# Opening order of an attention and two-MLP kernel: Q in one transfer, eight biased exponentials on ScalarE, halves of the last turned results

## The chip, the cores and the metric

The kernel runs on one core of a Trainium2 chip. The metric is the device time of one execution in microseconds, the lower the better; of several runs the median is given.

## The reference

Three layers follow one another. `q`, `k` and `v` have shape 4×8×768×64 (4 sequences, 8 heads), `mem_k` and `mem_v` 4×8×8×64; the first MLP has weights 512×2048 and 2048×512, the second the same sizes and one `alpha` for each hidden unit.

```python
for c in range(nc):                       # chunks of 32 queries
    c_start = c * chunk
    c_end = c_start + chunk
    l_start = max(0, c_start - left_ctx)  # 16 keys to the left
    r_end = min(S, c_end + right_ctx)     # 8 to the right
    k_full = np.concatenate([mem_k, k_ctx], axis=2)
    v_full = np.concatenate([mem_v, v_ctx], axis=2)
    scores = scale * np.matmul(q_c, k_full.transpose(0, 1, 3, 2))
    scores = scores - np.max(scores, axis=-1, keepdims=True)
    a = np.exp(scores)
    a = a / (np.sum(a, axis=-1, keepdims=True) + 1e-09)
    out[:, :, c_start:c_end] = np.matmul(a, v_full)
...
h = x @ w_in                              # 3072 x 512 by 512 x 2048
g = np.maximum(h, 0.0) + np.log1p(np.exp(-np.abs(h)))
x = (g @ w_out)
...
g = np.maximum(h, 0.0) + alpha * np.minimum(h, 0.0)
return (g @ w_out)
```

## The kernel before

**Attention.** The 3072 rows (sequence by position) are cut into 24 tiles of 128 rows; a tile is four chunks of 32 queries, for all 8 heads. Tiles 0 to 3 make the first block of 512 rows, tiles 4 to 7 the second; these eight are the *early* tiles, and tiles 8 to 23 (`few` in the code) are loaded in another way. One tile t goes through these steps, whose numbers stand behind the letters in what follows (s3 is the scores of tile 3):

- load of Q and K (`load_q`, `load_k`, into a room `qk`) and of V (`load_v`, six transfers: two halves of the columns, each from three ranges of rows, the memory's among them); all of them from the queue of SyncE (SP);
- q: for early tiles the heads of Q are put in the order that the scores want (`a_order`, two copies on ScalarE, here qa and qb). Half of each operand has to be zero, since two heads share a multiplication (the host lays Q out with these zeros); before the change `others` fills that half with `memset` (on VectorE for tile 0, on GpSimd for the other early tiles);
- s: 32 small matrix products on TensorE into the PSUM bank `ps_s`;
- m: the row maximum on VectorE (`a_max`, `nm`); then either the shift by it on VectorE (`a_shift`) and e, the exponential of 128×512 on ScalarE (`a_exp`), or, where a switch asks for it, `a_bias` on VectorE (the negative maximum, 128×8) and `a_shifted_exp`, eight exponentials of 128×64 on ScalarE, each with its own bias;
- the sum, the reciprocal and w, the share of each key (`a_share`, on VectorE or GpSimd);
- t: four transposes on TensorE into `ps_t`, and pt, their copies to SBUF on ScalarE;
- x: 32 products with V into `ps_x`, and from there xh on ScalarE and xl on VectorE: the two parts, high and low, into which each fp32 operand of the MLPs is split so that three fast products make one exact one.

**First MLP.** It goes by groups of one block and 128 hidden units: H (`pe_h`) is 12 matrix products of 128×512 into `ps_hh`; ScalarE computes ta and the high part of g (`act_first`, `high`), VectorE its low part (`low`); O (`pe_out`) is 12 products into `ps_o`. For the exponentials of the attention and for ta ScalarE loads different tables (ACT_TABLE_LOAD). The weights come in 512 KB rooms `raw`, and each is split into high and low parts: wh on ScalarE, wl on VectorE or GpSimd.

**Second MLP.** It is done by seven products in place of eight of quartered matrices (`quad`, `second`, bank `ps_q`); at the end VectorE turns results (`flip`: a transpose of each half and four stores).

**What sets the order.** For the first part `schedule` describes each step as a task of a `Plan` (engine, estimated microseconds, a due time, what it needs, what rooms it takes); `Plan.run` lists the tasks by due time as engines come free. The due times come from a table of numbers `O`, which also holds switches (`by0`, `by1`: GpSimd computes shares; `ca0`, `ca1`: the biased exponentials for tiles 0 to 3 and 4 to 7; `wld`: how many early wl go to VectorE). Each engine then runs its instructions strictly in that order (`InOrder`), and the same holds for loads: a load is an instruction in the queue of the engine that issues it. In the built program each load carries one of eight semaphores (DMAHW0 to DMAHW7), and a load waits on its issuing engine until an earlier load on that semaphore has landed.

Of the kernel before, what the change touches and what calls it, by code (L numbers as in the profile page):

```python
# [31 lines left out]
QN = 2 * NPAIR * P  # L32
# [48 lines left out]

PLAN = []
RUNS = 8
O = {'qo': 19.43, 'km': 103.61, 's': 132.4, 'm': 86.98, 'c': -51.87, 'e': 175.6, 'n': -19.49, 'r': -46.35, 'w': -19.52, 't': 95.77, 'pt': 85.42, 'v': 4.11, 'xh': -85.13, 'xl': -37.52, 'first': 4.43, 'gap': 13.49, 'second': 13.8, 'gap2': 10.89, 'raw': 76.14, 'ab': -97.97, 'cl': -24.77, 'ca': -41.63, 'cb': -28.14, 'cc': -52.39, 'wh': 1.69, 'wl': -37.29, 'odd': 61.8, 'sp': 29.0, 'hi': -84.66, 'lo': 120.66, 'out': 14.22, 'wait': 0.06, 'sloads': 10.35, 'qo0': 31.77, 'qo1': 59.63, 'km0': 45.44, 'km1': -1.09, 's0': 33.53, 's1': 68.06, 'm0': 99.26, 'm1': -29.86, 'c0': 87.42, 'c1': 86.99, 'e0': -47.46, 'e1': 46.23, 'n0': 20.17, 'n1': -4.91, 'r0': 23.19, 'r1': -6.49, 'w0': -81.15, 'w1': -23.28, 't0': 107.79, 't1': -40.96, 'pt0': 0.74, 'pt1': -5.53, 'v0': -87.68, 'v1': 71.52, 'xh0': -18.53, 'xh1': -22.32, 'xl0': 2.53, 'xl1': 34.49, 'by0': 3.34, 'by1': 1.01, 'va': -80.0, 'vb': -248.8, 'vc': -188.24, 'vd': -121.62, 'ra': -92.44, 'rb': -99.39, 'rc': -59.46, 'wld': -3.93, 'dra': -16.84, 'qpd': -4.87, 'ca0': 0.43, 'ca1': -2.85}


class Plan:
# [16 lines left out]
    def run(self):  # L104
# [10 lines left out]
        while left:  # L115
            able, first = [], 1e9
            for name, since in ready.items():
                engine, us, due, _, _, take, _, _ = left[name]
                t = max(since, free.get(engine, 0.0) if engine else 0.0, now)
                if engine == "SP":  # L120
                    t = max(t, free.get("DMA", 0.0) - 4.0)
                for r in set(take):
                    short = take.count(r) - rooms[r]
                    if short > 0:
                        later = sorted(u for u, g in back if g == r)
                        t = max(t, later[short - 1] + self.LAG if len(later) >= short else 1e9)
                able.append((t, due, name, engine))
            t, _, chosen, engine = min(able, key=lambda x: x[:2])
            if engine == "DMA":
                chosen = min((x for x in able if x[3] == "DMA"), key=lambda x: ready[x[2]])[2]  # L130
            if t >= 1e9:
                PLAN[:] = [x[:4] for x in order]
                raise ValueError([x[2] for x in able])
            now = t
            if engine and engine != "DMA":
                near = [x for x in able if x[3] == engine and x[0] < t + O["wait"]]
                if engine == "PE" and self.beside(last_pe):
                    near = [x for x in near if self.beside(x[2])] or near
# [12 lines left out]
            for u, g in [x for x in back if x[0] <= t]:
                rooms[g] += 1
                back.remove((u, g))
            if tab and tab != table:
                us, table = us + 1.3, tab
            if engine == "PE":
                if self.beside(name) and self.beside(last_pe):
                    us -= 0.24
                last_pe = name
                if t < 90.0 and t - free.get("PE", 0.0) > 0.5:  # L160
                    self.idle[name] = (max(free.get("PE", 0.0), came), t)
            if engine == "DVE" and free.get("POOL", 0.0) > t:
                us += 0.25 * min(us, free["POOL"] - t)
            done[name] = t + us
            if engine:
                free[engine] = t + us
            back += [(t + us, g) for g in give]
            order.append((t, us, engine, name, work))
            for a in then.get(name, ()):
                wants[a] -= 1  # L170
                if not wants[a]:
                    ready[a] = max(done[b] for b in left[a][4]) + self.LAG
# [4 lines left out]
def attention_mlp_mlp_kernel(ctx: ExitStack, tc, qk, v, w1, w2, consts, out):  # L177
# [159 lines left out]
    def load_q(t, e, c=None):  # L337
        part = slice(e * D, (e + 1) * D)
        rows = qk[t][part, :QN].rearrange("p (n e k) -> p n e k", e=2, k=D)[:, :, e]
        if c is None:  # L340
            sp.dma_start(out=raw_q[t][part].rearrange("p (n k) -> p n k", k=D), in_=rows)
        else:
            sp.dma_start(out=own(q_t[t], e)[:, c], in_=rows[:, :, c * CHUNK:(c + 1) * CHUNK])

# [9 lines left out]
        else:  # L354
            v_t[t] = apool.tile([P, 2 * DM], F32, tag="v", name="v", bufs=1)

    def load_v(t):
        for u, to, at, n in (
            (0, 0, MEM0, NMEM), (0, NMEM, 0, KW - NMEM), (0, KW, CHUNK, KW),
            (1, 0, 0, KW), (1, KW, SW - KW + NMEM, KW - NMEM), (1, 2 * KW - NMEM, MEM0 - D, NMEM),  # L360
        ):
            part = slice(u * DM, (u + 1) * DM)
            sp.dma_start(out=v_t[t][to:to + n, part], in_=v[t][at:at + n, part])

    def a_order(t, e, other=False):

        (dve.tensor_copy if other else act.copy)(out=own(q_t[t], e), in_=raw_q[t][e * D:(e + 1) * D].rearrange("p (n c k) -> p c n k", c=2, k=CHUNK))

    score_ps, turned, x_ps, part_of = {}, {}, {}, {}

# [395 lines left out]
            result(1, part)  # L766
            turn(c[:, 1, part], 1, 2 * h, 2, (lambda o, i: act.copy(out=o, in_=i), dve.tensor_copy)[h], (act, sp)[h])

    def flip(c, b, d):

        rows = out[b * N2:(b + 1) * N2, d * HK:(d + 1) * HK].rearrange("(c i) (m a j) -> m a i c j", i=32, m=2, j=32)
        for m in range(2):
            o = c[:, m, :].rearrange("p (c i) -> p c i", i=32)
            dve.transpose(out=o, in_=o)
            for a in range(4):
# [7 lines left out]
    def second(p, todo):  # L783
# [34 lines left out]
        for n in range(7 * NQ):  # L818
# [42 lines left out]
                    later.pop(0)()  # L861
            elif later:
                later.pop(0)()
            if (i, q) in ((4, 7), (5, 6), (6, 5)):
                d, b = ((0, 1), (1, 1), (0, 0))[i - 4]
                flip(c.pop((d, b)), 2 * p + b, d)
            for piece in todo.get(n, ()):
                piece()
            if 7 * NQ - n in (12, 8, 4, 1):
# [37 lines left out]
    def schedule(when):  # L907
# [5 lines left out]
        def nothing():  # L913
            pass

        def dma(name, issue, move, due, work, after=(), take=(), give=(), eng="SP"):
            add(("i",) + name, eng, issue, due, work, after, take)
            add(("x",) + name, "DMA", move, due, nothing, [("i",) + name])
            add(name, "", 2.0, due, nothing, [("x",) + name], [], give)

        for n, k in enumerate(order):
            f = k // 2
# [12 lines left out]
        for i, (b, f, first, final) in enumerate(steps):  # L935
# [10 lines left out]
            if final:  # L946
# [5 lines left out]
                for m in range(4):  # L952
                    by_act = m % 2 == 0 or f < HALF and O["dra"] > 0.5
                    add(("dr", i, m), "ACT" if by_act else "DVE", 0.65, t + 12.6, lambda i=i, m=m, b=b, by_act=by_act: drain_one(0 if by_act else 1, acc[b][m], staged[i][:, m, :]), [("db", i)], [], ["acc"])
                    dma(("dd", i, m), 1.1 if adds else 0.4, 1.0 if adds else 0.8, t + 16, lambda i=i, m=m, b=b, adds=adds: drain_to(m, staged[i][:, m, :], b, adds),
                        [("dr", i, m)], eng="POOL" if adds else "SP")
# [9 lines left out]
        def tile(t, prev, due, step=None):  # L966
# [12 lines left out]
            soon = -100 + 2 * t if start else due - O["sloads"]  # L979
            add(("qr", t), "", 0.0, soon, room, free_qk, qrooms)  # L980
            def load(c=None):
                for e in range(2):
                    load_q(t, e, c)
            if few:
                for c in range(2):
                    dma(("q", t, c), 1.5, 0.9, soon, lambda c=c: load(c), [("qr", t)] + ([("i", "q", t, c - 1)] if c else []))
            else:
                dma(("qk", t, 2), 1.45, 2.7, soon, lambda: (load(), load_k(t)), [("qr", t)])
            kafter = [("i", "q", t, 1)]
            if few:  # L990
# [190 lines left out]
```

## Time and profile before

| | |
|---|---|
| device time, 3 runs | 1090.9 us median (1090.0 to 1092.84) |
| the profiled execution | 1089.11 us, of which the span is 1087.1 us |
| mean granted clock of TensorE | 0.994 |
| TensorE busy | 1066.3 us, 98% of the span |
| VectorE / ScalarE / GpSimd busy | 717.6 / 559.7 / 232.9 us |

The span goes from the first to the last instruction that the profiler recorded; what lies around it (2.0 us here) is start and end. The profile has no program lines that help (each operation passes through line 71), so its rows are told apart by the names of the tiles. In the rows v is the room of a tile's shares and operands (it holds ordered Q, then the shifted scores and V), `word` the weight on its way to its parts, `SPq` the queue of SyncE.

### The profile page before, as it was taken

Reading aid. Unit: us, or ns where it says so; the run is one execution under the profiler, and the core shown is the slowest. Engines: PE = TensorE matmul, PEld = TensorE weight load, DVE = VectorE, ACT = ScalarE, POOL = GpSimd, SP = SyncE. Lnnn points to the kernel's source line nnn. Section 1 sums busy time; section 2 is a strip of 40 time slices with the busy share of each in tenths; the row PEclk is TensorE's granted clock in tenths of the full one; section 3 lists DMA queues with packets and bytes.
Section 4 is the critical chain, followed back from the end, with each engine's and each line's share of the span. In section 5 each row is a group of like instructions: output and inputs, shape, how many; then the busy total and the mean of one; then the engine's idle time right before and its main releaser. Section 6 shows DMA issues by size and latency. Waiting matters only on the chain.

```text
span 1087.1 us, 16452 instructions
## 1 busy us (share of the span) xinstructions
PE 1066.3 (98%) x6003; PEld 874.6 (80%) x6003; DVE 717.6 (66%) x1150; ACT 559.7 (51%) x974; POOL 232.9 (21%) x281
## 2 busy tenths in 40 slices
PE   7799999999999999999999999999999999999998
PEld 4578878888888888888888888888888888888886
DVE  6799989566644544444358166778666779666976
ACT  5654335465563554353244355765455665456543
POOL 4444444424123332223233400000000000000000
PEclk9899999999999999999999999999999999999999
DMA  9955674768644465444356373799874999856904
GB/s 225 234 152 185 167 187 121 187 164 215 186 127 151 153 197 137 167 118 151 111 194 225 134 304 113 293 276 318 201 275 174 335 300 255 239 223 252 370 1 78
DMA packets 173839, 214.53 MB, mean 197 GB/s; under 512 B 96064, under 2 KB 125888, under 8 KB 166848
## 3 DMA queue, kind: packets, MB, share of 16 engines
q1 hardware_dynamic: 169456, 196.59, 56.6%
q0 software_dynamic: 4032, 16.78, 7.9%
q8 instruction: 47, 0.77, 0.3%
q14 instruction: 32, 0.26, 0.1%
q10 hardware_dynamic: 272, 0.13, 0.0%
HBM read 154.74 MB, written 46.14 MB: 185 GB/s over the span
## 4 chain that ended last, share of the span: by engine, by line
PE 94%; DVE 3%; DMA 2%; SPq 1%; ACT 0%; issue 0%; DVEq 0%; ACTq 0%
PE ps_q L71 41%; PE ps_o L71 24%; PE ps_hh L71 24%; PE ps_x L71 2%; PE ps_s L71 2%; DVE word L71 1%; DMA raw<-in_w_dram 1%; PE ps_t L71 1%; SPq L71 1%; DMA wout<-out_ops 1%; DMA qk<-in_qk_dram 0%; DVE sm L71 0%; DVE x L71 0%; DVE nm L71 0%; DVE v L71 0%
## 5 line engine op out<-in xcount | busy, mean ns | idle before, releaser
L71 PE MATMUL ps_hh<-x,wsplit 128*128 128x512 f32 x1152 | 280.2, 392 | 0.6 <-DVE x L71 0.5
L71 PE MATMUL ps_o<-g,wsplit 128*128 128x512 f32 x1152 | 279.4, 391 | 0.8 <-ACT ta L71 0.7
L71 PEld LDWEIGHTS ps_o<-g,wsplit 128*128 128x128 f32 x1152 | 215.0, 188 | 46.5 <-ACT ta L71 1.1
L71 PEld LDWEIGHTS ps_hh<-x,wsplit 128*128 128x128 f32 x1152 | 214.5, 188 | 45.7 <-DVE x L71 0.8
L71 PE MATMUL ps_q<-g,wout 128*128 128x512 f32 x1008 | 229.3, 389 | 0.1
L71 PE MATMUL ps_q<-xop,win 128*128 128x512 f32 x1008 | 229.2, 389 | 0.0
L71 PEld LDWEIGHTS ps_q<-g,wout 128*128 128x128 f32 x1008 | 189.1, 188 | 39.8 <-ACT gb L71 0.5
L71 PEld LDWEIGHTS ps_q<-xop,win 128*128 128x128 f32 x1008 | 189.2, 188 | 39.4
L71 DVE TENSOR_TENSOR g<-ta,g 128x512 fp32r<-128x512 f32 x96 | 71.8, 748 | 132.3 <-ACT g L71 132.1
L71 ACT CAST g<-gb 128x512 fp32r<-128x512 f32 x168 | 100.8, 622 | 88.5 <-PE ps_q L71 64.6
L71 DVE TENSOR_TENSOR g<-gb,g 128x512 fp32r<-128x512 f32 x168 | 114.3, 687 | 37.9 <-ACT g L71 36.2
L71 ACT CAST g<-ta 128x512 fp32r<-128x512 f32 x96 | 59.6, 621 | 147.8 <-PE ps_o L71 147.6
L71 ACT ACTIVATE ta<-ps_hh 128x512 f32<-128x512 f32 x96 | 57.4, 598 | 106.3 <-PE ps_hh L71 101.9
L71 DVE SCALAR_TENSOR_TENSOR word<-raw,word 128x512 int32<-128x512 int32 x128 | 106.3, 831 | 2.5
L71 ACT ACTIVATE tp<-gb 128x512 f32<-128x512 f32 x48 | 30.4, 633 | 91.8 <-DVE gb L71 91.8
L71 POOL TENSOR_TENSOR wst<-wsum,wst 128x512 fp32r<-128x512 f32 x32 | 42.3, 1321 | 124.6 <-ACT wst L71 124.6
L71 POOL DMA_DIRECT2D gb<-gb x12 | 10.5, 874 | 263.6 <-DVE g L71 176.1
L71 DVE TENSOR_SCALAR word<-word 128x512 f32<-128x512 f32 (+1 forms) x128 | 65.0, 512 | 1.8
L71 POOL TENSOR_TENSOR wsplit<-word,wsplit 128x512 fp32r<-128x512 f32 x32 | 48.9, 1531 | 64.7 <-ACT wsplit L71 58.1
L71 DVE SCALAR_TENSOR_TENSOR gb<-gb,tp 128x512 f32<-128x512 f32 x48 | 33.2, 692 | 44.0 <-ACT tp L71 44.0
L71 POOL TENSOR_TENSOR wst<-word,wst 128x512 fp32r<-128x512 f32 (+1 forms) x32 | 37.6, 1176 | 110.7 <-ACT wst L71 110.7
L71 DVE TENSOR_SCALAR word<-raw 128x512 int32<-128x512 int32 x64 | 39.0, 610 | 32.0 <-POOL wst L71 13.6
(81 smaller groups left out, 930.9 us busy)
## 6 DMA issues: line engine op xcount, KB each, us to landing
wout<-out_ops SPq DMA_DIRECT2D x42, 1024.0 KB
raw<-in_w_dram SPq DMA_DIRECT2D x64, 512.0 KB
win<-in_ops SPq DMA_DIRECT2D x24, 1024.0 KB
win<-in_ops SPq DMA_DIRECT2D x24, 768.0 KB
out_ops<-wst SPq DMA_DIRECT2D x56, 256.0 KB
in_ops<-wst SPq DMA_DIRECT2D x24, 512.0 KB
gb<-gb POOLq DMA_DIRECT2D x12, 1024.0 KB, 13.5
v<-in_v_dram SPq DMA_DIRECT2D x48, 128.0 KB
```

Of the source, the lines that this page charges most:

```text
L71: i = getattr(self.engine, name)(*args, **kw)
```

## The change

The table `O` is replaced, and with it the order of the first part; of its switches four change their effect: tiles 4 to 7 take the eight biased exponentials on ScalarE in place of shift and one exponential; the shares of tiles 4 to 7 go to VectorE, not GpSimd; the first four wl go to VectorE, not GpSimd; and the six V loads of tiles 2 and 7 are issued from ScalarE's queue. For early tiles Q is loaded with one transfer of 128×1024 numbers (512 KB, the zeros that the host laid out included) where two transfers of 64×8×64 (128 KB each) brought the numbers alone; `others` is no longer called, and `a_order` copies 128×512 in place of 64×512. Some of the planner's costs differ. At the end the last turned result of each pair of blocks is stored in halves, two steps earlier.

```diff
-O = {'qo': 19.43, ..., 'by0': 3.34, 'by1': 1.01, ..., 'wld': -3.93, ..., 'ca0': 0.43, 'ca1': -2.85}
+O = {'qo': 1.94, ..., 'by0': 1, 'by1': 0, ..., 'wld': 4, ..., 'ca0': 0, 'ca1': 1, ..., 'vq2': 1, ..., 'vq7': 1, 've': 19.65}
...
-            if engine == "DVE" and free.get("POOL", 0.0) > t:
-                us += 0.25 * min(us, free["POOL"] - t)
+            if engine == "DVE":
+                us *= 0.88
+                if free.get("POOL", 0.0) > t:
+                    us += 0.3 * min(us, free["POOL"] - t)
...
-            raw_q[t] = room[:, :QN // 2]
+            raw_q[t] = room[:, :QN]
...
-            sp.dma_start(out=raw_q[t][part].rearrange("p (n k) -> p n k", k=D), in_=rows)
+            sp.dma_start(out=raw_q[t], in_=qk[t][:, :QN])
...
-    def load_v(t):
+    def load_v(t, queue):
...
-            sp.dma_start(out=v_t[t][to:to + n, part], in_=v[t][at:at + n, part])
+            queue.dma_start(out=v_t[t][to:to + n, part], in_=v[t][at:at + n, part])
...
-        (dve.tensor_copy if other else act.copy)(out=own(q_t[t], e), in_=raw_q[t][e * D:(e + 1) * D].rearrange("p (n c k) -> p c n k", c=2, k=CHUNK))
+        (dve.tensor_copy if other else act.copy)(out=q_t[t][:, e], in_=raw_q[t].rearrange("p (n c k) -> p c n k", c=2, k=CHUNK)[:, e])
...
-            if (i, q) in ((4, 7), (5, 6), (6, 5)):
-                d, b = ((0, 1), (1, 1), (0, 0))[i - 4]
-                flip(c.pop((d, b)), 2 * p + b, d)
+            for at, half, d, b in ((39, 0, 0, 1), (39, 1, 0, 1), (46, 0, 1, 1), (46, 1, 1, 1), (50, 0, 0, 0), (51, 1, 0, 0)):
+                if n == at:
+                    flip(c[d, b], 2 * p + b, d, [half])
...
-            dma(("v", t), 2.9, 2.0, (O["va"], O["vb"], O["vc"], O["vd"])[t] if start else due - 24, lambda: load_v(t), [("vr", t)])
+            by_act = not few and O["vq%d" % t] > 0.5
+            dma(("v", t), 3.0, 2.0, (O["va"], O["vb"], O["vc"], O["vd"])[t] if start else due - (24 if few else O["ve"]), lambda: load_v(t, act if by_act else sp), [("vr", t)], eng="ACT" if by_act else "SP")
...
-                add(("qz", t), "POOL" if t else "DVE", 1.5 if t else 1.1, (-50, 0)[t > 0] + t, lambda: others(q_t[t], pool if t else dve), [("vr", t)])
```

SyncE, from the program's start, before. The rooms qk_97 to qk_100 are those of tiles 0 to 3, v_119 that of tile 0:

```order
L71 DMA qk_97<-in_qk_dram 64x8x64 x2
L71 DMA qk_97<-in_qk_dram 128x4x160
L71 DMA qk_98<-in_qk_dram 64x8x64 x2
L71 DMA qk_98<-in_qk_dram 128x4x160
L71 DMA cst<-in_consts_dram 128x144
L71 DMA qk_99<-in_qk_dram 64x8x64
L71 DMA qk_99<-in_qk_dram 64x8x64 [waits DMAHW0_49]
L71 DMA qk_99<-in_qk_dram 128x4x160 [waits DMAHW1_49]
```

The same place of the changed kernel, as far as the first weights (`raw`); v_117 is the room of tile 0:

```order
L71 DMA qk_97<-in_qk_dram 128x1024
L71 DMA qk_97<-in_qk_dram 128x4x160
L71 DMA qk_98<-in_qk_dram 128x1024
L71 DMA qk_98<-in_qk_dram 128x4x160
L71 DMA cst<-in_consts_dram 128x144
L71 DMA qk_99<-in_qk_dram 128x1024
L71 DMA qk_99<-in_qk_dram 128x4x160
L71 DMA qk_100<-in_qk_dram 128x1024
L71 DMA qk_100<-in_qk_dram 128x4x160 [waits DMAHW0_49]
...
L71 DMA v_117<-in_v_dram 8x512 [waits DMAHW6_49]
L71 DMA raw<-in_w_dram 128x512 [waits DMAHW7_49]
```

A tile's Q and K are two instructions now, not three, and the first `raw` waits for the load on DMAHW7, which is Q of tile 3 (the eighth load).

ScalarE, from the exponential of tile 0 on, before:

```order
L71 ACTIVATE v_119<-v_119 128x512 [waits DVE_49,PE_49]
L71 COPY v_171<-qk_98 64x16x32 [waits DMAHW4_49]
L71 COPY v_196<-qk_99 64x16x32 [waits DMAHW7_49]
L71 COPY v_196<-qk_99 64x16x32 [waits DMAHW0_49]
L71 COPY pt<-ps_t 64x8x32 [waits PE_49]
L71 COPY pt<-ps_t 64x8x32 x3
L71 COPY v_255<-qk_100 64x16x32 [waits DMAHW2_49]
L71 ACTIVATE v_171<-v_171 128x512 [waits DVE_49]
```

And in the changed kernel (v_203 is tile 2, v_163 tile 1, v_223 tile 3):

```order
L71 ACTIVATE v_117<-v_117 128x512 [waits DVE_49,PE_49]
L71 DMA v_203<-in_v_dram 8x512 [waits DMAHW1_49]
L71 DMA v_203<-in_v_dram 56x512 [waits DMAHW3_49]
L71 DMA v_203<-in_v_dram 64x512 [waits DMAHW5_49]
L71 DMA v_203<-in_v_dram 64x512 [waits DMAHW7_49]
L71 DMA v_203<-in_v_dram 56x512 [waits DMAHW1_49]
L71 DMA v_203<-in_v_dram 8x512 [waits DMAHW3_49]
L71 COPY v_203<-qk_99 128x512
L71 ACTIVATE v_163<-v_163 128x512 [waits DVE_49,PE_49,Activation_49]
L71 COPY v_203<-qk_99 128x512
L71 COPY v_223<-qk_100 128x512
L71 COPY pt<-ps_t 64x8x32 [waits PE_49]
```

Six loads of V now stand ahead of the exponential of tile 1. The fourth of them waits on DMAHW7 for the first `raw`; the fifth and the sixth wait on DMAHW1 and DMAHW3 for the first and the second of the six themselves.

ScalarE, ahead of the second block's tiles, before: the exponential of tile 4 (v_357) is one instruction.

```order
L71 ACTIVATE v_357<-v_357 128x512 [waits DVE_49,PE_49,Activation_49]
L71 ACT_TABLE_LOAD
L71 ACTIVATE ta<-ps_hh 128x512 [waits PE_49]
L71 CAST g<-ta 128x512 [waits Activation_49]
L71 COPY v_483<-qk_419 64x16x32 [waits DMAHW3_49]
L71 COPY v_483<-qk_419 64x16x32 [waits DMAHW4_49]
```

The same place of the changed kernel (v_339 is tile 4, v_399 tile 5, v_483 tile 6, v_544 tile 7):

```order
L71 ACTIVATE v_339<-ps_s,nm 128x64 [waits DVE_49,PE_49,Activation_49]
L71 ACTIVATE v_339<-ps_s,nm 128x64 x7
L71 DMA v_544<-in_v_dram 8x512 [waits DMAHW0_49,Pool_49]
L71 DMA v_544<-in_v_dram 56x512 [waits DMAHW2_49]
L71 DMA v_544<-in_v_dram 64x512 [waits DMAHW4_49]
L71 DMA v_544<-in_v_dram 64x512 [waits DMAHW6_49]
L71 DMA v_544<-in_v_dram 56x512 [waits DMAHW0_49]
L71 DMA v_544<-in_v_dram 8x512 [waits DMAHW2_49]
L71 COPY v_483<-qk_376 128x512
L71 ACTIVATE v_399<-ps_s,nm 128x64 [waits DVE_49,PE_49,Activation_49]
L71 ACTIVATE v_399<-ps_s,nm 128x64 x7
```

Eight exponentials stand for one, and behind them the six loads of V of tile 7, the fifth and sixth again behind the first and second of their own. TensorE's order hardly differs: in both kernels all eight early tiles, four H and one O come ahead of the second O, and from there on the order is the same kind of alternation.

## Rows read from the trace of the kernel before

**Rows 1.** Windows: stretch, us, then busy time of PE, PEld, DVE, ACT, POOL, PEclk, DMA share, GB/s.

```profile
10.00:20.00 10.00, 6.68 (x134) 5.76 (x134) 5.62 (x13) 6.45 (x13) 4.23 (x15) 0.83 1.06 246
40.00:50.00 10.00, 6.34 (x74) 5.30 (x73) 7.15 (x17) 6.08 (x11) 1.98 (x4) 0.66 0.97 243
70.00:80.00 10.00, 10.00 (x46) 8.27 (x45) 9.54 (x15) 3.23 (x6) 4.18 (x3) 1.00 0.48 156
1000.00:1060.00 60.00, 60.00 (x267) 49.64 (x266) 50.25 (x82) 30.93 (x54) 0.00 (x0) 1.00 0.50 203
```

**Rows 2.** Timeline of TensorE: start, us, work, count, idle time before and its releaser.

```profile
34.20 2.83 PE L71 MATMUL ps_hh<-x,wsplit 128*128 128x512 f32 x11 [0.54 <-DVE x L71]
44.47 1.11 PE L71 MATMUL ps_t<-cst,v 128*128 128x128 f32 x4 [3.39 <-POOL v L71]
59.71 0.66 PE L71 MATMUL ps_t<-cst,v 128*128 128x128 f32 x4
65.11 3.00 PE L71 MATMUL ps_hh<-x,wsplit 128*128 128x512 f32 x12
68.04 1.15 PE L71 MATMUL ps_x<-pt,v 128*64 128x64 f32 x32
69.12 1.19 PE L71 MATMUL ps_o<-g,wsplit 128*128 128x512 f32 x4
```

**Rows 3.** Timeline of ScalarE.

```profile
3.82 0.62 ACT L71 COPY v<-qk 64x512 f32<-64x512 f32 x1 [1.79 <-DMA qk<-in_qk_dram]
9.52 0.63 ACT L71 ACTIVATE v<-v 128x512 f32<-128x512 f32 x1 [2.13 <-DVE v L71]
15.19 1.51 ACT L71 COPY pt<-ps_t 64x256 f32<-64x256 f32 x4 [3.12 <-PE ps_t L71]
17.26 0.62 ACT L71 ACTIVATE v<-v 128x512 f32<-128x512 f32 x1
37.40 1.28 ACT L71 ACT_TABLE_LOAD   x1
38.70 0.60 ACT L71 ACTIVATE ta<-ps_hh 128x512 f32<-128x512 f32 x1
```

**Rows 4.** Timeline of SyncE's queue: when its loads are issued, and for how long.

```profile
0.75 4.06 SPq L71 DMA_DIRECT2D qk<-in_qk_dram  x6
9.66 3.04 SPq L71 DMA_DIRECT2D v<-in_v_dram  x6
```

**Rows 5.** The chain that ended last, to 70 us: start, us, transfer waited for.

```profile
13.11 5.05 DMA raw<-in_w_dram
35.95 5.08 DMA raw<-in_w_dram
```

**Rows 6.** DMA issues: what, count, size of one.

```profile
qk<-in_qk_dram SPq DMA_DIRECT2D x16, 128.0 KB
```

**Rows 7.** Timelines of VectorE and GpSimd in the opening.

```profile
8.73 0.69 DVE L71 TENSOR_TENSOR v<-ps_s,nm 128x512 f32<-128x512 f32 x1
41.55 0.43 DVE L71 TENSOR_SCALAR word<-raw 128x512 int32<-128x512 int32 x1 [4.92 <-DMA v<-in_v_dram]
12.15 1.17 POOL L71 MEMSET v<- 64x256 f32 x4
```

**Rows 8.** Timelines of VectorE and TensorE behind the opening: the 15th low part and its O.

```profile
135.24 0.68 DVE L71 TENSOR_TENSOR g<-ta,g 128x512 fp32r<-128x512 f32 x1
140.37 2.88 PE L71 MATMUL ps_o<-g,wsplit 128*128 128x512 f32 x12
```

**Rows 9.** The page's costliest groups: a step of the splitting of weights, two for each of 64.

```profile
L71 DVE SCALAR_TENSOR_TENSOR word<-raw,word 128x512 int32<-128x512 int32 x128 | 106.3, 831 | 2.5
```

**Rows 10.** Timeline of the tail: SyncE's and ScalarE's queues and ScalarE.

```profile
1078.64 4.15 SPq L71 DMA_DIRECT2D out_dram<-c  x8
1081.89 0.89 ACT L71 COPY o_sb<-ps_q 128x512 f32<-128x512 f32 x2 [4.74 <-PE ps_q L71]
1082.89 1.05 SPq L71 DMA_DIRECT2D out_dram<-o_sb  x2
```

More of the change, by code (lines that the diff above doesn't have):

```diff
@@ L83 @@
 RUNS = 8
-O = {'qo': 19.43, 'km': 103.61, 's': 132.4, 'm': 86.98, 'c': -51.87, 'e': 175.6, 'n': -19.49, 'r': -46.35, 'w': -19.52, 't': 95.77, 'pt': 85.42, 'v': 4.11, 'xh': -85.13, 'xl': -37.52, 'first': 4.43, 'gap': 13.49, 'second': 13.8, 'gap2': 10.89, 'raw': 76.14, 'ab': -97.97, 'cl': -24.77, 'ca': -41.63, 'cb': -28.14, 'cc': -52.39, 'wh': 1.69, 'wl': -37.29, 'odd': 61.8, 'sp': 29.0, 'hi': -84.66, 'lo': 120.66, 'out': 14.22, 'wait': 0.06, 'sloads': 10.35, 'qo0': 31.77, 'qo1': 59.63, 'km0': 45.44, 'km1': -1.09, 's0': 33.53, 's1': 68.06, 'm0': 99.26, 'm1': -29.86, 'c0': 87.42, 'c1': 86.99, 'e0': -47.46, 'e1': 46.23, 'n0': 20.17, 'n1': -4.91, 'r0': 23.19, 'r1': -6.49, 'w0': -81.15, 'w1': -23.28, 't0': 107.79, 't1': -40.96, 'pt0': 0.74, 'pt1': -5.53, 'v0': -87.68, 'v1': 71.52, 'xh0': -18.53, 'xh1': -22.32, 'xl0': 2.53, 'xl1': 34.49, 'by0': 3.34, 'by1': 1.01, 'va': -80.0, 'vb': -248.8, 'vc': -188.24, 'vd': -121.62, 'ra': -92.44, 'rb': -99.39, 'rc': -59.46, 'wld': -3.93, 'dra': -16.84, 'qpd': -4.87, 'ca0': 0.43, 'ca1': -2.85}
+O = {'qo': 1.94, 'km': 27.02, 's': 68.65, 'm': 37.21, 'c': -21.27, 'e': 72.99, 'n': 2.46, 'r': 23.71, 'w': 26.89, 't': 3.69, 'pt': 12.88, 'v': 48.43, 'xh': 36.4, 'xl': -7.67, 'first': 3.02, 'gap': 5.83, 'second': 22.01, 'gap2': 5.07, 'raw': 16.56, 'ab': -50.96, 'cl': 12.94, 'ca': 41.62, 'cb': -47.47, 'cc': -20.06, 'wh': -8.39, 'wl': -5.23, 'odd': 36.26, 'sp': 43.97, 'hi': -36.62, 'lo': 61.09, 'out': 11.57, 'wait': 0.03, 'sloads': 48.37, 'qo0': 18.95, 'qo1': 57.05, 'km0': 64.56, 'km1': 87.87, 's0': 43.12, 's1': 87.34, 'm0': 33.94, 'm1': 11.79, 'c0': -0.57, 'c1': 23.14, 'e0': 12.58, 'e1': 74.44, 'n0': -31.26, 'n1': 44.06, 'r0': 3.97, 'r1': -25.42, 'w0': -19.33, 'w1': -34.53, 't0': -0.59, 't1': 46.61, 'pt0': -1.03, 'pt1': 62.4, 'v0': -27.31, 'v1': 34.96, 'xh0': -21.84, 'xh1': 32.14, 'xl0': 31.54, 'xl1': -0.07, 'by0': 1, 'by1': 0, 'va': -60.66, 'vb': -60, 'vc': -67.7, 'vd': -60, 'ra': -82.17, 'rb': -118.31, 'rc': -110.64, 'wld': 4, 'dra': 0, 'qpd': 0, 'ca0': 0, 'ca1': 1, 'vq0': 0, 'vq1': 0, 'vq2': 1, 'vq3': 0, 'vq4': 0, 'vq5': 0, 'vq6': 0, 'vq7': 1, 've': 19.65}
 class Plan:
@@ L159, in run @@
                 last_pe = name
+                if t > 90.0 and t - free.get("PE", 0.0) > 2.0:
+                    us += 1.6
                 if t < 90.0 and t - free.get("PE", 0.0) > 0.5:
                     self.idle[name] = (max(free.get("PE", 0.0), came), t)
-            if engine == "DVE" and free.get("POOL", 0.0) > t:
-                us += 0.25 * min(us, free["POOL"] - t)
+            if engine == "DVE":
+                us *= 0.88
+                if free.get("POOL", 0.0) > t:
+                    us += 0.3 * min(us, free["POOL"] - t)
             done[name] = t + us
@@ L767, in ending, with flip @@
             turn(c[:, 1, part], 1, 2 * h, 2, (lambda o, i: act.copy(out=o, in_=i), dve.tensor_copy)[h], (act, sp)[h])
-    def flip(c, b, d):
+    def flip(c, b, d, halves=range(2)):
         rows = out[b * N2:(b + 1) * N2, d * HK:(d + 1) * HK].rearrange("(c i) (m a j) -> m a i c j", i=32, m=2, j=32)
-        for m in range(2):
+        for m in halves:
             o = c[:, m, :].rearrange("p (c i) -> p c i", i=32)
@@ L914, in nothing, with dma @@
             pass
-        def dma(name, issue, move, due, work, after=(), take=(), give=(), eng="SP"):
+        def dma(name, issue, move, due, work, after=(), take=(), give=(), eng="SP", land=2.0):
             add(("i",) + name, eng, issue, due, work, after, take)
             add(("x",) + name, "DMA", move, due, nothing, [("i",) + name])
-            add(name, "", 2.0, due, nothing, [("x",) + name], [], give)
+            add(name, "", land, due, nothing, [("x",) + name], [], give)
         for n, k in enumerate(order):
@@ L954, in schedule @@
                     add(("dr", i, m), "ACT" if by_act else "DVE", 0.65, t + 12.6, lambda i=i, m=m, b=b, by_act=by_act: drain_one(0 if by_act else 1, acc[b][m], staged[i][:, m, :]), [("db", i)], [], ["acc"])
[L955 to L956 removed]
+                    dma(("dd", i, m), 1.2 if adds else 0.4, 2.2 if adds else 0.8, t + 16, lambda i=i, m=m, b=b, adds=adds: drain_to(m, staged[i][:, m, :], b, adds),
+                        [("dr", i, m)], eng="POOL" if adds else "SP", land=4.0 if adds else 2.0)
                 add(("ds", i), "", 0.0, 0, nothing, [("dd", i, m) for m in range(4)], [], room if f < HALF else [])
@@ L981, in load @@
             def load(c=None):
-                for e in range(2):
+                for e in range(2 if few else 1):
                     load_q(t, e, c)
@@ L987, in tile @@
             else:
-                dma(("qk", t, 2), 1.45, 2.7, soon, lambda: (load(), load_k(t)), [("qr", t)])
+                dma(("qk", t, 2), 1.2, 2.9, soon, lambda: (load(), load_k(t)), [("qr", t)])
             kafter = [("i", "q", t, 1)]
@@ L992, in tile @@
             add(("vr", t), "", 0.0, soon + 2, lambda: room_v(t), [("i", "qk", t, 2)] + ([("i", "v", prev)] if prev >= 0 else []), vrooms)
-            dma(("v", t), 2.9, 2.0, (O["va"], O["vb"], O["vc"], O["vd"])[t] if start else due - 24, lambda: load_v(t), [("vr", t)])
+            by_act = not few and O["vq%d" % t] > 0.5
+            dma(("v", t), 3.0, 2.0, (O["va"], O["vb"], O["vc"], O["vd"])[t] if start else due - (24 if few else O["ve"]), lambda: load_v(t, act if by_act else sp), [("vr", t)], eng="ACT" if by_act else "SP")
             queries = [("q", t, c) for c in range(2) if few or c]
             if not few:
-                add(("qz", t), "POOL" if t else "DVE", 1.5 if t else 1.1, (-50, 0)[t > 0] + t, lambda: others(q_t[t], pool if t else dve), [("vr", t)])
-                add(("qo", t), "ACT", 0.6, due - when_due("qo"), lambda: a_order(t, 0), [("qk", t, 2), ("qz", t)])
+                add(("qo", t), "ACT", 0.6, due - when_due("qo"), lambda: a_order(t, 0), [("qk", t, 2), ("vr", t)])
                 other = start and O["qpd"] > 0.5
-                add(("qp", t), "DVE" if other else "ACT", 0.5 if other else 0.6, due - when_due("qo"), lambda: a_order(t, 1, other), [("qo", t)])
+                add(("qp", t), "DVE" if other else "ACT", 0.7 if other else 0.6, due - when_due("qo"), lambda: a_order(t, 1, other), [("qo", t)])
                 queries = [("qp", t)]
```

## Prediction

> **What bounds the kernel now.** I read the windows first, to see where TensorE is not full. From 70 us on it is: 10.00 of 10 us, and 60.00 of 60 us near the end [rows 1]. In the opening it isn't: 6.68 and 6.34 of 10 us in two stretches, and the granted clock there is 0.83 and 0.66, that is, part of the time at 1.2 GHz instead of 2.4 [rows 1]. So a change of the opening's order can move the end only by moving the moment from which TensorE is full. The timeline of TensorE gives it: the second O begins at 69.12 us [rows 2]. By then the eight early tiles, four H and one O are done, in both kernels, and nothing that follows is less work in one than in the other. I therefore forecast the start of this second O, call it T, and move the end by the same amount. The profiled execution took 1089.11 us, 1.8 under the median of 1090.9; the shift of T is added to the median.
>
> What holds the opening back? In ScalarE's timeline it waits 3.12 us for transposes, and the exponential of tile 1 comes at 17.26 [rows 3]. The chain of waits passes over the transfers of `raw`, 5.05 and 5.08 us long, issued at 13.11 and 35.95 [rows 5]; the late second kind leaves VectorE idle for 4.92 us and after it TensorE for 3.39 us [rows 7, 2]. The DMA engines are full (share 1.06 and 0.97 at 246 and 243 GB/s) [rows 1]. So loads, VectorE and ScalarE take turns, and ScalarE has few reserves once it is made to wait.
>
> **The change, part by part: the first V loads on ScalarE.** The new order puts the six loads of tile 2's V between the exponentials of tiles 0 and 1. The exponential of tile 0 ends at 10.15 before [rows 3], and I leave it there. A load costs its engine 3.04/6 = 0.51 us to issue [rows 4]. The fourth load waits until the first `raw` has landed, and that is issued only after Q of tile 3 has landed. Before, the first `raw` goes out at 13.11 and takes 5.05 us, which gives 18.16 [rows 5]; with Q's bytes doubled I keep this time. Then three more issues (the fifth and the sixth wait for loads that landed by then): ScalarE is free at 18.16 + 1.5 = 19.7. If nothing had to be waited for, it would be free at 10.15 + 6 × 0.51 = 13.2: the two ends. I take the upper one, because the wait is on a transfer that has a row.
>
> From 19.7 ScalarE goes through nine steps up to the copies of the first transposes and the first xh: the q copies and exponentials at 0.62 or 0.63, xh at 0.60 (as ta), pt 1.51 [rows 3]: 7 × 0.62 + 1.51 = 5.9, so 25.6. Then three pt, one exponential, two xh and one wh: 3 × 1.51 + 4 × 0.61 = 7.0, and some 2 us of waits for transposes between them (before, one such wait was 3.12; ScalarE is later now, so less): 34.6. Four more steps of 0.62 to xh of tile 3: 37.1. With a low part of 0.7 on VectorE of the same size [rows 8] the first H runs from 37.8, where before its main part started at 34.20 [rows 2]. This part costs 3.6 us at that point.
>
> **The eight exponentials.** No row has an ACTIVATE of 128×64. The nearest: one of 512 columns takes 0.62, a copy of 256 columns 1.51/4 = 0.38 [rows 3]. Eight at the rate of the columns alone are 0.62; eight at the price of 256 columns 3.0. The line through the two gives 0.14 + 0.00094 per column, 0.20 each, 1.6 for eight; with the step from a wait, 1.7. Before, the same step was 0.63, and VectorE did the shift in 0.69 [rows 7]. So ScalarE has 1.07 us more for each of four tiles, and VectorE saves about 0.5 each.
>
> The Trainium skill, "ScalarE: Activation LUTs", section "What ACT_TABLE_LOAD costs", gives an ACTIVATE with a bias operand per partition about 280 ns + 0.833 ns per column, and an overlap of 93 ns between neighbours: an estimate from that is 2.0 to 2.7 us for eight, and would make the sum below 1.2 to 4 us longer. Its figure without such an operand, 186 + 0.833 × 512 = 612 ns, agrees with the row of 0.62.
>
> **The second V loads, and the rest up to T.** From 37.1 I follow ScalarE, which hardly waits here. Q copies of tile 5 and a wh: 1.9, so 39.0; eight exponentials 1.7: 40.7; then the loads of tile 7's V, whose fifth waits for the landing of its own first. How long such a load takes from issue to landing lies between 3.07 us (the first load of all, issued at 0.75, used at 3.82 [rows 4, 3]) and 5.08 for 512 KB [rows 5]. I take 4.0, as this load is small but the DMA engines are full here. ScalarE is free two issues after that, at 45.7 (44.7 to 46.8). Then one q copy and the exponentials of tile 5, 48.0, pt 49.5, three more copies and a wh 52.0, xh 52.6, ta between two table loads at 1.28 each, 55.8, two times eight exponentials 59.2, g and pt 61.3, a table load and ta 63.2, xh and g 64.4, pt 66.0. Behind this pt TensorE still has t7, x6, H and x7 to do: 0.66 + 1.15 + 3.00 + 1.15 = 6.0 [rows 2]. T = 71.9 or so against 69.12: **+2.8**. Of the 3.6 us lost by the first H a part comes back, since the two waits of before (4.92 on VectorE, 3.39 on TensorE) have no cause in the new order: its `raw` loads go out earlier.
>
> **Q in one transfer.** Two transfers of 128 KB [rows 6] become one of 512 KB, so 8 × 256 KB = 2.1 MB more are moved in the opening. At 246 GB/s this is 8.5 us of transfer if bytes were the limit; below, it is a gain: SyncE spends 4.06 us on the six instructions of two tiles [rows 4], and needs four now, 1.35 us less for a pair. Rows of 4 KB take the place of rows of 256 bytes, so the transfer needs fewer packets. I take nothing for both together, with +6 and −2 as its ends. The GpSimd memsets of 1.17 us [rows 7] go. One stood ahead of the share of tile 0; worth up to 1.2 us there, but hidden behind ScalarE's stop: 0, and −1.2 as its end.
>
> **Shares and low halves.** Two weights are split earlier by the time of the 15th low part. That is 2 × 2 × 0.83 = 3.3 us at least [rows 9] more in front of it on VectorE; it had ended at 135.92, and its O began at 140.37 [rows 8]. The margin of 4.45 covers it: 0, up to +0.8.
>
> **The tail.** Eight stores hold SyncE from 1078.64 to 1082.79, and the last results, ready at 1082.78, are issued behind them [rows 10]. In halves two steps earlier these stores are out of the way: −0.2 (0 to −0.5).
>
> **Sum:** +2.8 − 0.2 = +2.6, rounded to +2.5 for the memsets: 1090.9 + 2.5 = **1093.4**.
>
> **The rivals.** *R1, faster: ScalarE is not held.* If the one Q transfer lands sooner (Q of tile 3 by 8 us instead of 13), the first `raw` is issued and landed earlier, and the loads on ScalarE cost only their issue. Then the first H keeps its 34.2 (−3.6), the second set of loads costs 3.0 instead of 5.0 (−2), T is 66.3 and the time 1087.8; with eight exponentials at the lower bound of 0.62 it is another 4.3 less, 1083.5. Middle: 1085.7. For it: SyncE's issue gets shorter and the waits of 4.92 and 3.39 go. Against it: the DMA share of 1.06. It decides from a landing of the first `raw` before 14.5 us.
>
> *R2, no change: the delay is absorbed.* ScalarE is held, but the time comes back completely: TensorE loses 3.39 us at 41 to 44 and runs partly at 1.2 GHz from 40 to 50 [rows 1, 2]; if it gets its work in a closer sequence there, the 2.8 are paid back: 1090.9. That the six loads on ScalarE don't do what moving them is to do belongs here. The Trainium skill, "DMA: Bandwidth & Descriptors", section "Issuing engines are not separate DMA queues", says that loads issued from another engine go over the same 16 DMA engines and only save time on the issuing sequencer; this trace's share of 1.06 agrees with that as far as it goes.
>
> *R3, slower: bytes bind.* If the 2.1 MB count at 246 GB/s, the loads up to tile 7 and the early `raw` come 8.5 us later, of which the gaps of before take 2 to 3: T about 75, that is 1090.9 + 5.9, about 1097. With eight exponentials at their upper end of 3.0 us in place of 1.7, and nothing else, it would be 1093.4 + 4 × 1.3 = 1098.6. For it: the DMA share of 0.97 to 1.06 in both stretches; against it: the opening's end (70 to 80 us) has a share of 0.48 only [rows 1].
>
> **How the numbers follow.** A difference below 0.3% (3.3 us: 1087.6 to 1094.2) is about what a measurement of this kernel can't tell from no change. Chances: my forecast 0.40, with its own range of 1091 to 1097.5; R1 0.28; R2 0.17; R3 0.15. Faster: 0.25 of R1 and 0.03 of R2, 0.28. Same: 0.03 of R1, 0.14 of R2, 0.21 of the forecast, 0.38. Slower: 0.19 of the forecast and R3, 0.34. The range must take in most of R1 and R3: 1084.5 to 1098.5 leaves out a quarter of R1 and of R3 and a little of the forecast, 0.15 to 0.2.
>
> **What would show it.** In the profile after, ScalarE should stand still from about 12 to 19.7 us in front of the exponential of tile 1 and for 2 us or more in the loads of tile 7; the eight exponentials should read 1.6 to 1.8 us; the first H should start at 38, the second O at 72. I am wrong if the first `raw` lands before 15 us, if ScalarE's idle time there is small, or if the granted clock between 10 and 50 us falls or rises by more than 0.1 against before, which moves T with no change of the order.

## The result, and the profile after

The changed kernel takes 1099.83 us (median of 6 runs, 1098.11 to 1103.93) against 1090.95 of the kernel before (6 runs). The ratio is 1.0083, with a 95% interval of 1.0068 to 1.0099: slower by about 9 us, outside my range of 1084.5 to 1098.5. The profiled execution is the longest of its runs, 1103.93 us with a span of 1101.9; a second profile of the same kernel, below, took 1101.78.

TensorE's timeline after, with the rows that answer to [rows 2]: the first stop, the first H, the second stop, and the second O, whose start I called T.

```profile
20.59 0.48 PE L71 MATMUL ps_s<-qk,v 128*64 128x64 f32 x2 [6.80 <-ACT v L71]
...
24.07 1.98 PE L71 MATMUL ps_x<-pt,v 128*64 128x64 f32 x32
...
40.13 3.41 PE L71 MATMUL ps_hh<-x,wsplit 128*128 128x512 f32 x12
...
59.35 0.58 PE L71 MATMUL ps_x<-zero 128*128 128x512 bf16 x1 [11.34 <-ACT v L71]
...
83.37 3.02 PE L71 MATMUL ps_o<-g,wsplit 128*128 128x512 f32 x12
```

T moved from 69.12 to 83.37, by 14.25 us, and this execution is 14.8 us longer than the one profiled before: the loss lies in the opening, as argued. Both long gaps of TensorE are put down to ScalarE (`ACT v`). ScalarE's timeline shows what it did there; an `ACTq` row gives the issues of loads from its queue, from the first to the last.

```profile
8.88 0.63 ACT L71 ACTIVATE v<-v 128x512 f32<-128x512 f32 x1
14.07 5.81 ACTq L71 DMA_DIRECT2D v<-in_v_dram  x6
19.92 0.62 ACT L71 COPY v<-qk 128x512 f32<-128x512 f32 x1 [10.41 <-DMA v<-in_v_dram]
...
25.38 0.63 ACT L71 ACTIVATE v<-v 128x512 f32<-128x512 f32 x1 [1.20 <-DVE v L71]
...
28.36 1.54 ACT L71 COPY pt<-ps_t 64x256 f32<-64x256 f32 x4 [1.67 <-PE ps_t L71]
...
41.62 1.74 ACT L71 ACTIVATE v<-ps_s,nm 128x64 f32<-128x64 f32 x8 [0.35 <-DVE nm L71]
49.34 7.65 ACTq L71 DMA_DIRECT2D v<-in_v_dram  x6
57.04 0.62 ACT L71 COPY v<-qk 128x512 f32<-128x512 f32 x1 [13.67 <-DMA v<-in_v_dram]
57.56 1.74 ACT L71 ACTIVATE v<-ps_s,nm 128x64 f32<-128x64 f32 x8
```

ScalarE stands for 10.41 us up to 19.92 and for 13.67 us up to 57.04 (the figure in brackets is its idle time up to the row's start). The first stop ends where the forecast had it (19.7); the second was to be 5.0 us. The windows, with the columns of [rows 1], show what is left of the other engines meanwhile, and that TensorE is as full as before near the end:

```profile
10.00:20.00 10.00, 2.60 (x20) 1.21 (x17) 1.75 (x5) 0.08 (x1) 1.75 (x5) 0.87 0.96 257
50.00:60.00 10.00, 0.58 (x1) 0.25 (x2) 0.67 (x2) 2.93 (x12) 0.00 (x0) 0.57 0.81 183
1000.00:1060.00 60.00, 60.00 (x266) 49.62 (x265) 46.59 (x74) 35.43 (x63) 0.00 (x0) 1.00 0.66 258
```

From 50 to 60 us TensorE works 0.58 us. Single issues, from the timelines of both queues: the first `raw` and the fourth load of the first set, then loads of the second set and those of SyncE that they wait for (the `qk` row is Q and K of tile 7; its second load goes out at 38.80).

```profile
12.92 0.36 SPq L71 DMA_DIRECT2D raw<-in_w_dram  x1
18.44 0.47 ACTq L71 DMA_DIRECT2D v<-in_v_dram  x1
...
38.33 0.91 SPq L71 DMA_DIRECT2D qk<-in_qk_dram  x2
...
43.44 0.28 SPq L71 DMA_DIRECT2D v<-in_v_dram  x1
46.92 0.27 SPq L71 DMA_DIRECT2D v<-in_v_dram  x1
49.34 0.29 ACTq L71 DMA_DIRECT2D v<-in_v_dram  x1
51.88 0.32 ACTq L71 DMA_DIRECT2D v<-in_v_dram  x1
53.72 0.61 ACTq L71 DMA_DIRECT2D v<-in_v_dram  x1
56.72 0.28 ACTq L71 DMA_DIRECT2D v<-in_v_dram  x1
```

The first load of tile 7's V shares its semaphore (DMAHW0) with the last of tile 5's, issued at 43.44: it goes out at 49.34, 5.9 us later. The second shares DMAHW2 with the first of tile 6's, issued at 46.92: it goes out at 51.88, 4.96 later. The sixth shares it with this second: 56.72, 4.84 later. So ScalarE waits for three landings, but the first two overlap: the end of the stop is set by the second and the third, one behind the other, and so by the moment at which SyncE issues the first load of tile 6's V. That load was held in the same way. SyncE had waited 1.1 us just before it for the K of tile 7, issued at 38.80 and also on DMAHW2: 8.1 us from one issue to the next. My sum had one landing, of 4.0 us.

### The profile page after: what moved, and what is told of

Read it like the earlier page. It is cut to its first block, busy times and chain, and to the rows that moved or that the text cites. A ratio compares the mean times of both kernels' runs of the same rounds, so it can differ in the third digit from the quotient of the medians.

```text
span 1101.9 us, 16382 instructions
## 1 busy us (share of the span) xinstructions
PE 1067.6 (97%) x5999; PEld 875.8 (79%) x6005; DVE 727.8 (66%) x1154; ACT 561.8 (51%) x1002; POOL 219.7 (20%) x245
## 4 chain that ended last, share of the span: by engine, by line
PE 89%; DVE 5%; DMA 3%; issue 1%; POOL 0%; ACT 0%; SPq 0%; ACTq 0%; DVEq 0%; POOLq 0%
PE ps_q L71 42%; PE ps_o L71 22%; PE ps_hh L71 21%; DVE word L71 3%; PE ps_x L71 2%; DMA raw<-in_w_dram 2%; PE ps_s L71 2%; DMA qk<-in_qk_dram 1%; PE ps_t L71 1%; POOL wsplit L71 0%; DMA qt<-in_qk_dram 0%; SPq L71 0%; DVE g L71 0%; ACT v L71 0%; DVE nm L71 0%
## 5 line engine op out<-in xcount | busy, mean ns | idle before, releaser
L71 DVE TENSOR_TENSOR g<-ta,g 128x512 fp32r<-128x512 f32 x96 | 76.4, 796 | 153.4 <-ACT g L71 153.2
L71 DVE SCALAR_TENSOR_TENSOR word<-raw,word 128x512 int32<-128x512 int32 x128 | 100.2, 783 | 2.9
L71 POOL TENSOR_TENSOR wst<-word,wst 128x512 fp32r<-128x512 f32 (+1 forms) x32 | 35.2, 1100 | 101.4 <-ACT wst L71 101.3
L71 DVE TENSOR_SCALAR word<-raw 128x512 int32<-128x512 int32 x64 | 42.1, 658 | 11.3 <-DMA raw<-in_w_dram 8.3
```

The source lines that it names most:

```text
L71: i = getattr(self.engine, name)(*args, **kw)
```

## The experiments

There are eleven further kernels (e1 to e11) and one more profile of the changed kernel (a0). In e1, e2, e3, e7, e8, e10 and e11 the order of the changed kernel is kept on every engine but for what is named; the loads that go back to SyncE stand there at the place that the plan gave them. T is read from one profiled execution and varies from one to the next: e6, whose opening is that of the kernel before, has 72.43 where that had 69.12. So kernels are compared by the medians of their times, and a difference of up to about 3 us in T alone says little.

**e1, e2, e3: who issues the V loads.** e1 takes tile 7's from ScalarE's queue, e2 tile 2's, e3 both.

```diff
-lambda: load_v(t, act if by_act else sp)
+lambda: load_v(t, act if by_act and t != 7 else sp)   # e1; e2: t != 2; e3: load_v(t, sp)
```

> The changed kernel with the six V loads of tile 7 issued from SyncE, all other instructions in the same order. Held-queue theory (ScalarE stands still because loads in its own queue wait for other loads to land): the stop of 13.7 us in front of the exponentials of tile 5 goes, the second O starts at about 74 us instead of 83.4, and the time falls by some 9 us to 1090 to 1092. Bytes theory (the 2.1 MB more of Q make every early load late, whoever issues it): the stop turns into waits for the same data elsewhere, the second O stays at 81 us or later, 1097 or more.

> The changed kernel with the six V loads of tile 2 issued from SyncE, those of tile 7 left on ScalarE. Held-queue theory: the exponential of tile 1 comes at about 13 us instead of 20.5 and the first H at 35 instead of 40.1, but the second stop, whose end is set by SyncE's loads of V of tiles 5 and 6, stays, so only 1 to 5 us come back: 1095 to 1099. Bytes theory: the exponential of tile 1 moves, the first H does not, 1099 to 1100.

> The changed kernel with all V loads issued from SyncE, all other instructions in the same order. Held-queue theory: both stops go, the second O starts at 66 to 70 us, 1086 to 1091. Bytes theory: second O at 78 or later, 1096 or more.

e1: 1092.51 us, ratio to before 1.0017 (1.0005 to 1.0029). e2: 1101.64, 1.0106 (1.0081 to 1.0132). e3: 1089.49, 0.9992 (0.9978 to 1.0005). So taking both sets off ScalarE gives the whole loss back (10.3 us), tile 7's alone 7.3, tile 2's alone nothing. The two do not add: once tile 7's are gone, tile 2's are worth 3.0 (e1 against e3). The second O in e1 and e2:

```profile
70.92 3.04 PE L71 MATMUL ps_o<-g,wsplit 128*128 128x512 f32 x12
79.41 3.02 PE L71 MATMUL ps_o<-g,wsplit 128*128 128x512 f32 x12
```

In e3 T is 67.31 (its row stands below), inside what I expected, as is its time. I expected 74 in e1, and 1090 to 1092, which its median passes by 0.5; the bytes theory, with 81 or later and 1097, is out. e2 came out worse than either theory had it (1095 to 1099, and 1099 to 1100). Its ScalarE timeline shows why the first set alone is worth nothing:

```profile
46.60 6.95 ACTq L71 DMA_DIRECT2D v<-in_v_dram  x6
53.59 0.62 ACT L71 COPY v<-qk 128x512 f32<-128x512 f32 x1 [15.59 <-DMA v<-in_v_dram]
```

ScalarE is there 5 us earlier (the first H starts at 35.10, not 40.13) and then stands 15.59 us instead of 13.67, until 53.59, where a0 below has 54.06: what is gained ahead of a wait whose end another queue sets is waited away.

**a0: the changed kernel again.** No edit.

> The changed kernel once more, unaltered, for a second profiled execution: the first took 1103.9 us where the median of its runs is 1099.8. Held-queue theory: what differs between executions is the length of ScalarE's second stop, since it hangs on when transfers land; an execution of about 1099 us shows a stop of 9 to 10 us instead of 13.7 and the second O at 78 to 80 instead of 83.4. Rival: the stop is as long, the second O within 1 us of 83.4, and the difference lies behind the opening.

1101.78 us, so not the execution of about 1099 that I had in mind. Its timelines of ScalarE and TensorE:

```profile
46.13 7.89 ACTq L71 DMA_DIRECT2D v<-in_v_dram  x6
54.06 0.62 ACT L71 COPY v<-qk 128x512 f32<-128x512 f32 x1 [11.04 <-DMA v<-in_v_dram]
...
80.39 3.02 PE L71 MATMUL ps_o<-g,wsplit 128*128 128x512 f32 x12
```

The stop is 11.04 us and T 80.39: 2.6 us less of the one, 3.0 less of the other, 2.2 less in time. In these two executions the time moves with the stop's length; the rival, a stop as long and the same T, is out.

**e10: tile 7's loads on ScalarE, but later.** On e3's ground; ScalarE issues them behind the exponentials of tile 7.

```diff
-lambda: load_v(t, sp), [("vr", t)]
+lambda: load_v(t, sp) if t != 7 else None, [("vr", t)]
...
-lambda: a_shifted_exp(t), [("c", t)]
+lambda: (a_shifted_exp(t), load_v(t, act) if t == 7 else None), [("c", t)]
```

> All V loads on SyncE but those of tile 7, which ScalarE issues 12 of its steps later, behind the exponentials of tile 7; order kept. If what costs is the waiting for other loads, and not that ScalarE issues: most of the loads waited for have landed by then, the six loads hold ScalarE for 3 to 6 us and not 11 to 14, second O at 68 to 73, 1090 to 1095. If loads on ScalarE stop it for as long wherever they stand: second O at 78 or later, 1099 or more.

1094.48 us, ratio 1.0037 (1.0024 to 1.0051), T 74.33 (1.3 us beyond what I gave). The timelines of ScalarE and TensorE:

```profile
57.08 3.82 ACTq L71 DMA_DIRECT2D v<-in_v_dram  x6
60.94 0.62 ACT L71 CAST g<-ta 128x512 fp32r<-128x512 f32 x1 [5.03 <-DMA v<-in_v_dram]
...
74.33 3.02 PE L71 MATMUL ps_o<-g,wsplit 128*128 128x512 f32 x12
```

The same six loads hold ScalarE for 5.03 us, not 11 to 14, and the kernel is 5.0 us above e3. Where the loads stand decides, since the waits differ; that ScalarE issues them at all costs up to 3.82 us here, from the first issue to the end of the last.

**e5, e6, e9: parts of the change alone, on the kernel before.** e5 loads Q in one transfer, with the copies of 128×512 that go with it, and drops the memsets, in the order of before (the fence shows the two loading lines and the memset; `nothing` is a function that does nothing); e6 stores the halves of the last turned results two steps earlier, with the lines of the change; e9 is both.

```diff
-            raw_q[t] = room[:, :QN // 2]
+            raw_q[t] = room[:, :QN]
...
-            sp.dma_start(out=raw_q[t][part].rearrange("p (n k) -> p n k", k=D), in_=rows)
+            sp.dma_start(out=raw_q[t], in_=qk[t][:, :QN])
...
-lambda: others(q_t[t], pool if t else dve)
+nothing
```

> The kernel before, its order kept, with Q of the eight early tiles in one transfer of 512 KB each (zeros included), copies of 128x512, and without the memsets of the zeros. Held-queue theory: the additional 2.1 MB cost little, because the packets are larger and SyncE issues less; second O at 67 to 70 us, 1089 to 1092. Bytes theory: second O at 73 to 76, 1095 to 1098.

> The kernel before with the last turned results stored in halves, two steps earlier, and nothing else. As forecast for the tail: 0.2 us less (0 to 0.5), which is inside what the runs can tell: 1090 to 1091.5. Rival: the earlier transposes stand in VectorE's way ahead of the last operands and TensorE waits: 1091.5 or more.

> The kernel before with two parts of the change alone: Q in one transfer (no memsets) and the halves of the last turned results; its order kept, all V loads on SyncE. If these two parts are the sound ones: second O at 66 to 67.5, 1088 to 1090. If the gain of the opening is given back behind it (VectorE has the same weights to split in less time): equal to before, 1090 to 1091.

e5: 1089.39 us, ratio 0.9999 (0.998 to 1.0017), T 66.57:

```profile
66.57 3.02 PE L71 MATMUL ps_o<-g,wsplit 128*128 128x512 f32 x12
```

In the order of before the 2.1 MB more cost nothing that can be seen; this is the run that decides against the bytes theory by itself (1095 to 1098). e6: 1090.69, 1.0002 (0.999 to 1.0015): not to be told from before, as expected. Its tail (the rows that answer to [rows 10]) shows the forecast's 0.2 as 0.4:

```profile
1086.69 0.89 ACT L71 COPY o_sb<-ps_q 128x512 f32<-128x512 f32 x2 [4.74 <-PE ps_q L71]
1087.30 1.08 SPq L71 DMA_DIRECT2D out_dram<-o_sb  x2
```

From the start of the copies to the issue it is 0.61 us, where it was 1.00. e9: 1088.07, 0.998 (0.9968 to 0.9992), the best median of all and inside the 1088 to 1090 expected of it. Its ratio is that of e7 and e8 below, and its interval overlaps that of e5, so whether it is better than these isn't shown. Its own profiled execution was the longest of its runs (1091.38, T 71.96), so its gain can't be placed in a row.

**e7, e8, e11: what VectorE, GpSimd and ScalarE exchange, on e3's ground.** e7: shift on VectorE and one exponential for tiles 4 to 7. e8: the shares of these tiles and the first four wl on GpSimd. e11: both.

```diff
-lambda: a_bias(t), [("m", t)]                        # e7, e11
+lambda: a_shift(t), [("m", t)]
-lambda: a_shifted_exp(t), [("c", t)]
+lambda: a_exp(t), [("c", t)]
...
-eng=dve if by_dve else pool: low_w(k, eng)           # e8, e11
+eng=pool: low_w(k, eng)
-lambda: a_share(t, pool if by_pool else dve)
+lambda: a_share(t, pool if by_pool or not few else dve)
```

> All V loads on SyncE, order kept, and tiles 4 to 7 with the shift on VectorE and one exponential of 128x512 instead of eight of 128x64. If ScalarE's longer step (1.74 against 0.63 us, four times) is what the eight pieces cost: the second O 1 to 4 us before the 67.3 of the run with eight pieces, 1086 to 1088.5. If VectorE is the tighter engine there (the shift costs it 0.5 us more for each tile): no gain or later, 1089.5 to 1092.

> All V loads on SyncE, order kept, and the shares of tiles 4 to 7 and the first four low halves of weights back on GpSimd. If VectorE is the tighter engine: TensorE's wait of 2 us for a low part at 70 to 73 us and the fall of the clock behind it go, 1086 to 1088. If GpSimd's longer steps (1.04 to 1.5 us against 0.7) are in the way of the first H and of the transposes: the second O later than 67.3, 1090 to 1093.

> The changed kernel's order with all V loads on SyncE, shares of tiles 4 to 7 and four low halves on GpSimd, and one exponential with the shift on VectorE: what is left of the change is the order, Q in one transfer and the halves. If the two gains seen singly (about 0.2% each) add: 1086 to 1088.5. If VectorE's splitting of weights behind the opening takes them back: 1089 to 1090.5.

1089.45 us (ratio 0.9982, 0.9968 to 0.9996), 1089.63 (0.9984, 0.9968 to 0.9999) and 1089.51 (0.9986, 0.9976 to 0.9996), against 1089.49 (0.9992) of e3: no difference that the runs can tell. T is 67.53, 66.66 and 67.36. In time the second expectation of e7 and that of e11 hold; that VectorE is the reason is not shown. e3's timeline of TensorE shows what is behind T there:

```profile
67.31 3.01 PE L71 MATMUL ps_o<-g,wsplit 128*128 128x512 f32 x12
70.47 0.49 PE L71 MATMUL ps_hh<-x,wsplit 128*128 128x512 f32 x1
72.94 3.94 PE L71 MATMUL ps_hh<-x,wsplit 128*128 128x512 f32 x11 [1.99 <-DVE x L71]
76.68 3.39 PE L71 MATMUL ps_o<-g,wsplit 128*128 128x512 f32 x12
```

TensorE waits 1.99 us for a low part from VectorE, and then runs at 1.2 GHz for some of the time: the window from 70 to 80 us has a granted clock of 0.83, and the H takes 3.94 us. In e7 and e8 this wait is 1.37 and 1.40, in e11 1.97, and in all three that window has a granted clock of 1.00. I expected e8 to remove the wait and the fall of the clock, if VectorE was the tighter engine; the wait got 0.6 us shorter, the clock did not fall, and the time stayed. Since e11 keeps its clock behind as long a wait, the wait alone does not decide the fall.

**e4: both switches at 0 and a new plan.** `'vq2': 1` and `'vq7': 1` become 0 in the table.

> The changed kernel with the two switches of the V loads at 0, so that its planner lays out an order for loads from SyncE alone. Held-queue theory: like the kept order with all loads on SyncE (1089.5) or up to 3 us better, since the plan fits: 1086 to 1090. Rival (the new table of numbers is worse by itself): 1092 or more.

1099.9 us, ratio 1.0072 (1.0043 to 1.01), T 76.75. The held-queue theory said 1086 to 1090 and missed; the rival, that the new table is worse by itself, holds for this plan. The loads don't stop ScalarE here. TensorE's timeline:

```profile
46.68 1.27 PE L71 MATMUL ps_s<-qk,v 128*64 128x64 f32 x32
53.60 0.61 PE L71 MATMUL ps_s<-zero 128*128 128x512 bf16 x1 [5.64 <-DVE x L71]
54.43 2.77 PE L71 MATMUL ps_s<-zero 128*128 128x512 bf16 x6 [0.22 <-issue]
57.12 1.98 PE L71 MATMUL ps_s<-qk,v 128*64 128x64 f32 x32
```

By this row it waits 5.64 us for a low part (`DVE x`) before it goes on to the scores of the next tile; VectorE itself had stood for a `raw` load shortly before, up to 48.67. The two switches change the whole order, not just who issues two sets of loads, so this run says nothing about the loads. Why that plan puts the low part so late was not tried.

## Why the prediction was wrong, step by step

- **T sets the end: right.** Time of the profiled execution minus T is 1020.0 before, 1020.6 after and 1021.4 in a0; in the other eleven kernels it lies between 1019.4 and 1023.0, while T goes from 66.6 to 79.4. The three highest (1022.8 to 1023.0, in e5, e3 and e11) belong to a T of 66.6 to 67.4: some of what an early T gains is given back behind it, by waits like that of e3.
- **The first V loads hold ScalarE until 19.7: right** (19.92). The first `raw` was issued at 12.92 and its landing let the fourth load go at 18.44. But the first H began at 40.13, not 37.8. For ScalarE's waits up to there my sum had 2 us, for transposes; they were 4.5 (1.20 and 1.67 in the rows above, and three of 0.44 to 0.61). How much of this is the low clock (0.62 from 20 to 30 us, where it was 1.00 before; TensorE had stood for 6.80 us) no run separates. (The steps that the text counts as nine are eight; the sum is that of eight.) What the first stop cost by itself is close to the 3.6 us forecast for it at the first H: e1 is 3.0 us above e3 in time (3.6 in T).
- **The second V loads: the step that failed.** It was "the loads of tile 7's V, whose fifth waits for the landing of its own first", 40.7 to 45.7. The waits of the first four, on SyncE's loads of V of tiles 5 and 6, had no term at all, although they stand in the order; only the own landing was priced. Measured: 43.36 to 57.04, 13.67 us (11.04 in a0) in place of 5.0. From there to T it was 26.3 us, where I had 26.2. The miss of T, 83.4 against 71.9, is 8.7 us of this term and 2.7 of the late arrival at it. That the term is the cause, and not a companion, is shown by e1, where only these six loads change their queue (7.3 us back), and e3.
- **Eight exponentials: right.** 1.74 us, forecast 1.7. One alone takes 0.33, and they overlap to 0.20 each. By the figures of the Trainium skill, "ScalarE: Activation LUTs", section "What ACT_TABLE_LOAD costs", an estimate for one is 280 + 0.833 × 64 = 333 ns, which the trace's mean of 328 ns bears out; with its overlap of 93 ns an estimate for the eight is 2.0 us, and the measured 1.74 decides for more overlap. Nor did the price matter: e7 takes the eight away and gains nothing.
- **Q in one transfer costs nothing: right** where the V loads stand on SyncE (e5, e3), and R3, that bytes bind, is out. Its 1097 came nearest to the measured time, by luck.
- **Tail: right in sign, too small to be seen** in the time (e6).
- **The rivals.** R1 and R2 assumed that the waits were over or paid back; they were not. The slower result came by the forecast's own mechanism, at a size that no rival had.

What stays open: how much the doubled Q lengthened the landings that ScalarE waited for, since no run has V loads on ScalarE with Q in two transfers (the DMA share was 0.96 and 0.81 in the windows of the two stops); why the K load in front of tile 6's V took some 8 us to land; and what e9's 0.2% comes from, if it is a gain.

## What to carry to other kernels

A load put on a compute engine's queue must be priced by when each load that shares its semaphore was issued, on whatever queue, plus its landing, and not by its own issue or landing: here six loads cost 5 us at one place (e10) and 11 to 14 at another. Follow every wait in the queue to the end, and ask which queue sets it; gains ahead of such a wait are lost in it (e2). If a table of numbers decides the order, test one part with the order held (e1, e3), since a new plan changes everything else as well (e4).

## What the runs showed of the hardware that was not expected

Three loads of 8 and 56 rows were waited for 4.8 to 5.9 us from their issue in the second stop, longer than the 3.07 us of the first load of all and nearly as long as a 512 KB transfer (5.50 us at 12.92). Twice the bytes of Q, in rows of 4 KB in place of 256 bytes, made the opening no slower in e5 (T 66.57, against 69.12). SyncE has fewer issues for it: in the changed kernel two tiles' Q and K take it 1.90 us instead of 4.06 [rows 4].
